# Exponential, row sum and maximum of eight softmaxes moved between two engines, head by head

## The chip, the cores and the metric

The kernel runs on one core of a Trainium2 chip. The metric is the device time of one execution in microseconds (us); the median of three timed runs is 855.88 us (855.29 to 855.99). One further execution was taken with a profile, and all rows below are from it. The engines are named as in the profile: PE is TensorE, DVE is VectorE, ACT is ScalarE, POOL is GpSimd, SP is SyncE. Differences within 0.2% (1.7 us) can't be told from no change.

## The reference, cut to what matters

```python
q_c, k_c, v_c = (x.reshape(B, H, nc, 64, D) for x in (q, k, v))   # B, H, S, D = 8, 8, 576, 64
scores = np.matmul(q_c, k_c.transpose(0, 1, 2, 4, 3)) / np.sqrt(D)
scores = scores - np.max(scores, axis=-1, keepdims=True)
attn = np.exp(scores)
attn = attn / (np.sum(attn, axis=-1, keepdims=True) + 1e-09)
x = np.matmul(attn, v_c)                  # then heads side by side: x is [4608, 512]
h = x @ w_in                              # w_in  [512, 2048]
g = np.maximum(h, 0.0) ** 2
out = g @ w_out                           # w_out [2048, 512]
```

Attention is done within chunks of 64 positions, so each chunk of a head has a softmax of its own over 64 scores. The two weight matrices come as 64-bit floats.

## The kernel before, in words

**Tiling.** Two chunks of all eight heads make a *pair*: 128 rows of `x`. There are 36 pairs, in blocks of 4, 4, 4, 6, 6, 6 and 6. The first eight pairs (class `Pair`; `NN` is 8) are the plain ones; the change touches these alone. The other 28 (class `Quad`) have a softmax of their own code. A value that goes into a large matmul is split in two parts, high and low, and each product takes three matmuls.

**A plain pair.** PE turns q and k (`turn`), and they are copied out of PSUM: q into the block-diagonal tile `qbd`, in two halves of 64 partitions (`keep_q`: by DVE for pairs 0 and 1, by ACT for the others), k into `kt` (`keep_k`, ACT). PE makes the scores in a PSUM bank, 128 rows by 8 heads by 64 (`scores`, tile `sc`). Then `top` (maximum per row and head, tile `nm`), `less` (scores less maximum, tile `ne`), `exps` (one exponential over all 512 columns, in place), `sums` (row sums, tile `nz`), `small` (adds 1e-9), `norm` (reciprocal and product). PE turns the result (`turn_p`), ACT copies it (`keep_p`, tile `tt`), PE multiplies by the values (`values`), ACT writes the high part of `x` and DVE the low part (`place`).

**The lead.** Pairs 0 to 3 are done first. Their `small` is on DVE, and they use banks of their own. Where PE has nothing to do in the lead, `fill` gives it runs of 8 or 16 short matmuls with no use (L393), as the 22 of `heat` at the start do. After pair 3 comes the first large matmul, slice `h0_0` of block 0.

**Block 0.** The first product has 16 slices (`h0_0` to `h0_15`), twelve matmuls each, and the second has 16 of twelve (`o0`), two slices behind (`LAG`). Each slice needs a converted piece of `w_in` or `w_out`: `convert_w` makes the split out of 64-bit words in seven steps, three instructions on ACT (L157, L158, L187) and five on DVE (L163, L169, L175, L182, L197), 32 pieces in all. So in the same stretch ACT and DVE convert weights, square and split `g` (ACT L617, L623, L629; DVE L632), and do the softmax of pairs 4 to 7 (`small` on POOL there).

**What sets the order.** `Plan` holds each step with an engine, a cost, what it reads and writes, and a rank; it plays the plan through with these costs and writes out each engine's instructions in that order. Engines then take their own queue in order and wait on semaphores. A changed cost or step therefore changes the order on every engine up to the end of block 0 and a little beyond.

Of the kernel before, what the change touches and what calls it, by code (L numbers as in the profile page):

```python
# [10 lines left out]
F32 = mybir.dt.float32  # L11
# [3 lines left out]
AF = mybir.ActivationFunctionType  # L15
ALU = mybir.AluOpType
AX = mybir.AxisListType
# [3 lines left out]
def kernel(  # L21
# [20 lines left out]
    nc = tc.nc  # L42
    B, H, S, D = q.shape
    NT, DM = out.shape
    DFF = w_in.shape[1] // 2
    P = 128
    CH = 64
# [4 lines left out]
    QSCALE = 1.0 / math.sqrt(D)  # L52
# [222 lines left out]
    class Quad:  # L275
# [31 lines left out]
        def less(self):  # L307
            self.e = late["pool"].tile([P, HH, 2, CH], F32, name=f"e{self.pair}", tag="e", bufs=1)
            for c in range(2):
                nc.vector.tensor_tensor(  # L310
                    self.e[:, :, c], four[c][:, 0], self.m[:, c].broadcast_to([P, HH, CH]), op=ALU.subtract
                )
# [4 lines left out]
        def sums(self):  # L317
            self.z = att.tile([P, HH, 2, 1], F32, name=f"z{self.pair}", tag="nz", bufs=2)
            nc.vector.tensor_reduce(self.z, self.e, axis=AX.X, op=ALU.add)
            nc.vector.tensor_scalar_add(self.z, self.z, 1e-9)  # L320
            nc.vector.reciprocal(self.z, self.z)
# [73 lines left out]
    class Pair:  # L395
# [36 lines left out]
        def keep_q(self, s):  # L432
            r = halves[s]

            copy = nc.vector.tensor_copy if self.u < 2 else nc.scalar.copy
            copy(qbd[self.u % 2][r, :, s], self.psq[r])

        def keep_k(self):
            self.kt = raw.tile([P, H, CH], F32, name=f"kt{self.u}", tag="qk"[self.u % 2] + "_raw")
# [12 lines left out]

        def top(self):
            self.m = att.tile([P, H, 1], F32, name=f"nm{self.u}", tag="nm", bufs=2)
            nc.vector.tensor_reduce(self.m, self.sc, axis=AX.X, op=ALU.max)

        def less(self):
            self.e = nat.tile([P, H, CH], F32, name=f"ne{self.u}", tag=f"ne{self.u % 2}")
            nc.vector.tensor_tensor(
                self.e, self.sc, self.m.broadcast_to([P, H, CH]), op=ALU.subtract  # L460
            )

        def exps(self):
            nc.scalar.activation(self.e, self.e, AF.Exp, scale=QSCALE)

        def sums(self):
            self.z = att.tile([P, H, 1], F32, name=f"nz{self.u}", tag="nz", bufs=2)
            nc.vector.tensor_reduce(self.z, self.e, axis=AX.X, op=ALU.add)

        def small(self):  # L470
            (nc.vector if self.lead else nc.gpsimd).tensor_scalar_add(self.z, self.z, 1e-9)
# [202 lines left out]
    class Mixed(Step):  # L674
# [30 lines left out]
        def add(self, i, h, side, s):  # L705
            nc.vector.tensor_tensor(self.kept(i)[:, h * HN:(h + 1) * HN], sides[side][:, :HN], snap(s), op=ALU.add)  # L706
# [246 lines left out]
    def program():  # L953
# [4 lines left out]
        add = p.add  # L958
# [41 lines left out]
        def attention(u):  # L1000
            x = prs[u]
            i = u % 2
            if x.lead:
                bq, bk, bs = ("o", 2 * i), ("o", 2 * i + 1), ("h", i)
            else:
                bq, bk, bs = (("at", next(turn_at) % 2) for _ in range(3))
            if 2 <= u < lead:
                bp, bx = bk, bq
            else:
                bp, bx = (("at", next(turn_at) % 2) for _ in range(2))  # L1010
            x.banks = {"q": bq, "k": bk, "sc": bs, "pt": bp, "xt": bx}
            r = ["early"]
            wait = 0.0 if x.lead else SLACK
            add(PE, 4 * 0.11, lambda: x.turn(0), [("q", u), "ident"], [bq], slack=wait)
            for s in range(2):
                e = DVE if u < 2 else ACT
                add(e, ONE, lambda s=s: x.keep_q(s), [bq] + r, [("qbd", i, s)])
            add(PE, 4 * 0.11, lambda: x.turn(1), [("k", u), "ident"], [bk], slack=wait)
            add(ACT, ONE, x.keep_k, [bk] + r, [("raw", "qk"[i])])
            if u in (0, lead - 1):  # L1020
                filler(x, "sc", bs, [bq, bk])
            add(PE, 1.05, x.scores, [("qbd", i, 0), ("qbd", i, 1), ("raw", "qk"[i])] + r, [bs],
                slack=wait)
            add(DVE, TWO, x.top, [bs], [("m", i)])
            add(DVE, TWO, x.less, [bs, ("m", i)] + r, [("e", i)])
            add(ACT, ONE, x.exps, r, [("e", i)])
            add(DVE, TWO, x.sums, [("e", i)] + r, [("z", i)])
            add(DVE if x.lead else POOL, 0.2 if x.lead else 0.41, x.small, [], [("z", i)])
            add(DVE, TWO + 0.2, x.norm, [("z", i)] + r, [("e", i)])
            if u in (0, lead - 1):  # L1030
                filler(x, "pt", bp, [bs])
            add(PE, 4 * 0.11, x.turn_p, [("e", i), "ident"] + r, [bp], slack=wait)
            add(ACT, ONE, x.keep_p, [bp] + r, ["tt"])
            if u in (0, lead - 2, lead - 1):
                filler(x, "xt", bx, [bp])
            add(PE, 1.05, x.values, [("v", slot_of(u)), "tt"] + r, [bx], slack=wait)
            xh, xl = x_names(u, "h"), x_names(u, "l")
            add(ACT, ONE, lambda: x.place(0), [bx], xh)
            add(DVE, TWO, lambda: x.place(1), [bx] + xh, xl)
# [416 lines left out]
```

## Time and profile before

| What | Value |
|---|---|
| median of three runs | 855.88 us |
| the profiled execution | 856.38 us, its span 854.6 us |
| PE busy | 845.0 us (99%) |
| DVE busy | 540.6 us (63%) |
| ACT busy | 367.8 us (43%) |
| POOL busy | 242.5 us (28%) |
| mean granted clock of PE | 0.999 |

The span runs from the first to the last instruction; 1.8 us of the profiled execution lie around it. The profiled execution is 0.5 us above the median. Busy shares are means over the whole span; the plain pairs lie in the first 116 us of it. A matmul's end is modelled in the profile, so PE's share says little by itself.

### The profile page before, as it was taken

The page shows a single profiled execution, that of the slowest core. Times are in us where ns is not written, and L with a number is a line of the kernel's source. Part 1 is how long each engine was busy: PE and PEld are TensorE (multiplying, and loading weights), DVE is VectorE, ACT ScalarE, POOL GpSimd, SP SyncE. Part 2 cuts the span into 40 slices and gives each one's busy share as a digit, 9 for nine tenths or more (in the row PEclk, how much of TensorE's full clock was granted, in tenths as well). Part 3 has the DMA queues.
Part 4 walks back from the last instruction along what each step waited for, and adds up shares of the span by engine and source line. Part 5 has one row for each costly group of instructions (what it writes and reads, how often), then busy time and mean ns, then how long its engine had stood idle before and what let it go on. Part 6 is the DMA issues. An engine that isn't in the chain of part 4 may idle for free.

```text
span 854.6 us, 16517 instructions
## 1 busy us (share of the span) xinstructions
PE 845.0 (99%) x6142; PEld 729.6 (85%) x6142; DVE 540.6 (63%) x962; ACT 367.8 (43%) x669; POOL 242.5 (28%) x432
## 2 busy tenths in 40 slices
PE   9999999999999999999999999999999999999998
PEld 7787878888888888888988988898898888999896
DVE  5999997777775347665586566566656637524233
ACT  4899885444454345232343323243332334222221
POOL 2000006344553122343331434342333222222110
PEclk9999999999999999999999999999999999999999
DMA  7797438666696326966784777674778443745311
GB/s 185 225 267 219 148 87 208 156 157 155 154 302 138 56 56 166 209 154 143 176 185 133 178 181 163 142 180 115 211 152 210 106 96 100 230 111 149 87 49 75
DMA packets 241504, 132.72 MB, mean 155 GB/s; under 512 B 185744, under 2 KB 200336, under 8 KB 241424
## 3 DMA queue, kind: packets, MB, share of 16 engines
q0 software_dynamic: 47360, 80.77, 35.1%
q1 hardware_dynamic: 191808, 50.24, 26.8%
q8 instruction: 49, 0.80, 0.4%
q10 hardware_dynamic: 2256, 0.66, 0.3%
q14 instruction: 31, 0.25, 0.1%
HBM read 103.81 MB, written 24.12 MB: 150 GB/s over the span
## 4 chain that ended last, share of the span: by engine, by line
PE 88%; DVE 10%; issue 1%; POOL 0%; ACT 0%; POOLq 0%; DVEq 0%
PE o L729 31%; PE side L697 28%; PE o L642 12%; PE h L606 11%; PE side L345 2%; PE side L298 2%; DVE wia L175 1%; DVE woa L175 1%; DVE wi L197 1%; DVE wia L182 1%; DVE woa L182 1%; DVE wo L197 1%; DVE wia L163 1%; DVE wia L169 1%; DVE gs L632 1%
## 5 line engine op out<-in xcount | busy, mean ns | idle before, releaser
L697 PE MATMUL side<-xc,ring 128*128 128x384 f32 x1344 | 241.3, 336 | 1.3 <-DVE xc L1240 1.3
L697 PEld LDWEIGHTS side<-xc,ring 128*128 128x128 f32 x1344 | 235.7, 188 | 4.9 <-DVE xc L1240 1.5
L687 POOL DMA_DIRECT2D ring<-combos x224 | 121.8, 544 | 311.1 <-PE side L697 304.0
L706 DVE TENSOR_TENSOR gf<-side,aside 128x384 f32<-128x384 f32 x96 | 53.5, 557 | 170.6 <-PE side L697 166.6
L606 PE MATMUL h<-x,wi 128*128 128x512 f32 x576 | 145.0, 395 | 1.6 <-ACT wi L187 1.0
L729 PE MATMUL o<-wo,gs_f 128*128 128x512 f32 x576 | 142.3, 395 | 0.0
L642 PE MATMUL o<-wo,gs 128*128 128x512 f32 x576 | 141.7, 392 | 0.0
L729 PE MATMUL o<-wo,gs_s 128*128 128x512 f32 x576 | 135.9, 389 | 0.0
L606 PEld LDWEIGHTS h<-x,wi 128*128 128x128 f32 x576 | 106.1, 188 | 26.6 <-DVE wi L197 2.7
L729 PEld LDWEIGHTS o<-wo,gs_s 128*128 128x128 f32 x576 | 108.1, 188 | 22.3
L642 PEld LDWEIGHTS o<-wo,gs 128*128 128x128 f32 x576 | 107.2, 188 | 22.3
L729 PEld LDWEIGHTS o<-wo,gs_f 128*128 128x128 f32 x576 | 106.5, 188 | 21.6
L272 POOL DMA_DIRECT2D v_raw<-in_v_dram x112 | 69.7, 633 | 106.8 <-PE side L345 80.5
L703 ACT COPY aside<-side 128x384 f32<-128x384 f32 x96 | 46.2, 481 | 120.7 <-PE side L697 120.2
L632 DVE TENSOR_TENSOR gs<-g,gs 128x512 fp32r<-128x512 f32 x48 | 32.9, 685 | 44.2 <-ACT gs L629 44.1
L712 DVE SCALAR_TENSOR_TENSOR gf<-gf 128x768 f32<-128x768 f32 x64 | 58.6, 952 | 1.1 <-ACT gf L709 0.9
L719 DVE TENSOR_TENSOR gs_f<-gf,gs_f 128x768 fp32r<-128x768 f32 x32 | 30.0, 937 | 23.7 <-ACT gs_f L715 23.7
L617 ACT ACTIVATE g<-h 128x512 f32<-128x512 f32 x48 | 28.6, 595 | 35.0 <-PE h L606 32.7
L629 ACT CAST gs<-g 128x512 fp32r<-128x512 f32 x48 | 29.7, 620 | 31.7 <-PE o L642 31.3
L709 ACT ACTIVATE gf<-side 128x384 f32<-128x384 f32 x32 | 15.7, 492 | 61.4 <-PE side L697 61.4
L305 DVE TENSOR_REDUCE m<-side 128x4 f32<-128x256 f32 x56 | 21.1, 418 | 30.5 <-ACT aside L357 28.6
L334 ACT COPY p<-et 128x512 f32<-128x512 f32 x28 | 17.4, 622 | 52.2 <-DVE et L328 51.9
(113 smaller groups left out, 846.9 us busy)
## 6 DMA issues: line engine op xcount, KB each, us to landing
ring<-combos POOLq DMA_DIRECT2D x224, 256.0 KB, 3.7
wiraw<-in_moe_w_in_dram SPq DMA_DIRECT2D x16, 512.0 KB, 6.1
woraw<-in_moe_w_out_dram SPq DMA_DIRECT2D x16, 512.0 KB, 5.8
out_dram<-ob SPq DMA_DIRECT2D x30, 256.0 KB, 3.3
q_raw<-in_q_dram SPq DMA_DIRECT2D x224, 32.0 KB, 2.1
k_raw<-in_k_dram SPq DMA_DIRECT2D x224, 32.0 KB, 3.6
v_raw<-in_v_dram POOLq DMA_DIRECT2D x112, 64.0 KB, 2.3
combos<-wi POOLq DMA_DIRECT2D x48, 128.0 KB, 3.1
```

The costliest lines, as they stand in the source:

```text
L272: nc.gpsimd.dma_start(out=t[r, c], in_=s.rearrange("h j d -> j h d"))
L606: nc.tensor.matmul(self.h[:, :self.n], a[:, c], bb[:, c, :self.n], start=c == 0 and i == 0, stop=last,)
L629: nc.scalar.copy(self.gh[:, :self.n], self.g)
L632: nc.vector.tensor_tensor(self.gl[:, :self.n], self.g, self.gh.bitcast(F32)[:, :self.n], op=ALU.subtract)
L642: nc.tensor.matmul(acc[b, j], a[:, j * P:(j + 1) * P], bb, start=f == 0 and i == 0, stop=f == NF - 1 and i == 2,)
L687: nc.gpsimd.dma_start(out=ring(self.m + i).rearrange("p l c n -> p (l c n)"), in_=combos[self.p, i])
L697: nc.tensor.matmul(sides[side][:, :HN], w[:, l, c], part(x, r)[:, c], skip_group_check=True, start=(c, u) == (0, 0) and i in (0, 1, 3), st ...
L703: nc.scalar.copy(snap(i), sides[side][:, :HN])
L706: nc.vector.tensor_tensor(self.kept(i)[:, h * HN:(h + 1) * HN], sides[side][:, :HN], snap(s), op=ALU.add)
L712: nc.vector.scalar_tensor_tensor(self.kept(i), self.kept(i), 0.0, self.kept(i), op0=ALU.max, op1=ALU.mult)
L719: nc.vector.tensor_tensor(l, self.kept(i), h.bitcast(F32), op=ALU.subtract)
L729: nc.tensor.matmul(acc[b, j], a[:, j * P:(j + 1) * P], bb, start=first and u == 0, stop=last and u == 2)
```

## The change: what it does

Of each plain pair, DVE's `less` and `sums` are taken out, two instructions over 128 rows and 512 columns. `exps` becomes eight instructions on ACT, one for each head, 128 rows by 64 columns: each reads the scores from PSUM, adds the head's maximum as a bias per row, takes the exponential, writes `ne`, and writes the row's sum to a column of `nz` (`accum_out`). So that bias and scores have the same scale, q is multiplied by -1/8 as it is copied (`keep_q`: a multiplication on DVE, an activation with a scale on ACT), and `top` takes the minimum of the negated scores. The planner's cost of `exps` goes from 0.61 to 8 times 0.21.

```diff
@@ keep_q
-            copy = nc.vector.tensor_copy if self.u < 2 else nc.scalar.copy
-            copy(qbd[self.u % 2][r, :, s], self.psq[r])
+            to, of = qbd[self.u % 2][r, :, s], self.psq[r]
+            if self.u < 2:
+                nc.vector.tensor_scalar_mul(to, of, -QSCALE)
+            else:
+                nc.scalar.activation(to, of, AF.Copy, scale=-QSCALE)
...
@@ top, less, exps, sums
-            nc.vector.tensor_reduce(self.m, self.sc, axis=AX.X, op=ALU.max)
-
-        def less(self):
+            nc.vector.tensor_reduce(self.m, self.sc, axis=AX.X, op=ALU.min)
+
+        def exps(self):
+
             self.e = nat.tile([P, H, CH], F32, name=f"ne{self.u}", tag=f"ne{self.u % 2}")
-            nc.vector.tensor_tensor(
-                self.e, self.sc, self.m.broadcast_to([P, H, CH]), op=ALU.subtract
-            )
-
-        def exps(self):
-            nc.scalar.activation(self.e, self.e, AF.Exp, scale=QSCALE)
-
-        def sums(self):
             self.z = att.tile([P, H, 1], F32, name=f"nz{self.u}", tag="nz", bufs=2)
-            nc.vector.tensor_reduce(self.z, self.e, axis=AX.X, op=ALU.add)
+            for h in range(H):
+                nc.scalar.activation(
+                    self.e[:, h], self.sc[:, h], AF.Exp, bias=self.m[:, h], scale=-1.0, accum_out=self.z[:, h]
+                )
...
@@ attention
             add(DVE, TWO, x.top, [bs], [("m", i)])
-            add(DVE, TWO, x.less, [bs, ("m", i)] + r, [("e", i)])
-            add(ACT, ONE, x.exps, r, [("e", i)])
-            add(DVE, TWO, x.sums, [("e", i)] + r, [("z", i)])
+            add(ACT, H * 0.21, x.exps, [bs, ("m", i)] + r, [("e", i), ("z", i)])
```

In the rows of order below, the digit in a tile's name is the pair (`kt1` is `kt` of pair 1), `side0`, `side1`, `pt` and `xt` are PSUM banks, and a row with x8 stands for eight equal instructions.

On ACT in the lead, from `keep_k` of pair 0 on, before:

```order
L440 COPY kt0_179<-k0_161 128x512
L440 COPY kt1_220<-k1_204 128x512
L464 ACTIVATE ne0_226<-ne0_226 128x512
L436 COPY qbd0_93<-q2_228 64x8x64 x2
L440 COPY kt2_275<-k2_259 128x512
L436 COPY qbd1_94<-q3_270 64x8x64
L491 COPY tt0_303<-side0_80 128x512
L436 COPY qbd1_94<-q3_270 64x8x64
L464 ACTIVATE ne1_301<-ne1_301 128x512
L440 COPY kt3_324<-k3_306 128x512
L464 ACTIVATE ne2_348<-ne2_348 128x512
```

and now:

```order
L443 COPY kt0_179<-k0_161 128x512
L465 ACTIVATE ne0_220,nz0_221<-sc0_166,nm0_202 128x64 x8
L443 COPY kt1_240<-k1_204 128x512
L439 ACTIVATE qbd0_93<-q2_235 64x8x64 x2
L443 COPY kt2_275<-k2_242 128x512
L490 COPY tt0_288<-side0_80 128x512
L465 ACTIVATE ne1_307,nz1_308<-sc1_251,nm1_281 128x64 x8
L439 ACTIVATE qbd1_94<-q3_283 64x8x64
L465 ACTIVATE ne2_358,nz2_359<-sc2_290,nm2_322 128x64 x8
...
L439 ACTIVATE qbd1_94<-q3_283 64x8x64
L443 COPY kt3_401<-k3_317 128x512
```

The eight instructions of pair 0 stand ahead of `kt1`, which the scores of pair 1 need; those of pairs 1 and 2 stand ahead of `kt3`, which the scores of pair 3 need.

On PE in the lead, from the values of pair 0 on (the rows left out are runs of L393), before:

```order
L500 MATMUL side1_81<-tt0_303,vbd0_95 64x64 x16
...
L448 MATMUL sc3_354<-kt3_324,qbd1_94 64x64 x16
L486 MATMUL side0_80<-ident_88,ne1_301 128x128 x4
...
L500 MATMUL side1_81<-tt1_411,vbd1_96 64x64 x16
L486 MATMUL pt2_444<-ident_88,ne2_348 128x128 x4
```

and now:

```order
L499 MATMUL side1_81<-tt0_288,vbd0_95 64x64 x16
L485 MATMUL side0_80<-ident_88,ne1_307 128x128 x4
...
L485 MATMUL pt2_394<-ident_88,ne2_358 128x128 x4
...
L499 MATMUL side1_81<-tt1_388,vbd1_96 64x64 x16
L451 MATMUL sc3_372<-kt3_401,qbd1_94 64x64 x16
...
L499 MATMUL xt2_403<-tt2_477,vbd2_97 64x64 x16
L485 MATMUL pt3_483<-ident_88,ne3_514 128x128 x4
```

The scores of pair 3 (`sc3`) now stand behind the turned results of pairs 1 and 2 and the values of pair 1, where before they stood ahead of all three. The last row, `pt3`, turns the result of pair 3.

On DVE in block 0, around the softmax of pair 4, before:

```order
L455 TENSOR_REDUCE nm4_763<-side0_80 128x8
L163 TENSOR_SCALAR woa3_753<-woa3_753 128x512
L459 TENSOR_TENSOR ne4_772<-side0_80,nm4_763 128x512
L169 TENSOR_SCALAR woa3_753<-woa3_753 128x512
L163 TENSOR_SCALAR wia5_765<-wia5_765 128x512
L175 SCALAR_TENSOR_TENSOR woa3_753<-woraw3_507,woa3_753 128x512
L169 TENSOR_SCALAR wia5_765<-wia5_765 128x512
L468 TENSOR_REDUCE nz4_791<-ne4_772 128x8
L182 ISA woa3_753<-woraw3_507,woa3_753 128x1024
L474 RECIPROCAL nz4_791<-nz4_791 128x8
```

and now:

```order
L458 TENSOR_REDUCE nm4_789<-side0_80 128x8
L197 TENSOR_TENSOR wi4_783<-wia4_706,wi4_783 128x512
L175 SCALAR_TENSOR_TENSOR woa3_757<-woraw3_525,woa3_757 128x512
L182 ISA woa3_757<-woraw3_525,woa3_757 128x1024
L163 TENSOR_SCALAR wia5_796<-wia5_796 128x512
L169 TENSOR_SCALAR wia5_796<-wia5_796 128x512
L175 SCALAR_TENSOR_TENSOR wia5_796<-wiraw5_528,wia5_796 128x512
L631 TENSOR_TENSOR gs0_3_826<-g0_3_780,gs0_3_826 128x512
L473 RECIPROCAL nz4_807<-nz4_807 128x8
L474 TENSOR_TENSOR ne4_806<-ne4_806,nz4_807 128x512
L197 TENSOR_TENSOR wo3_833<-woa3_757,wo3_833 128x512
```

Between the maximum and the reciprocal of pair 4, DVE now has seven instructions of weights and of `g`, and neither L459 nor L468; the reciprocal waits for POOL's addition, and this for the last of ACT's eight heads. Behind it stands the last step of `wo3`.

## Rows read from the trace of the kernel before

**Rows 1.** Busy us of each engine in three stretches of the first 116 us.

```profile
core 0: us, PE busy (x) PEld busy (x) DVE busy (x) ACT busy (x) POOL busy (x), PEclk, DMA share, GB/s
5.00:31.35 26.35, 25.20 (x382) 21.48 (x380) 21.68 (x43) 15.80 (x29) 1.65 (x2) 1.00 0.83 226
31.35:41.36 10.01, 8.86 (x37) 6.71 (x37) 9.94 (x20) 9.20 (x17) 0.00 (x0) 1.00 0.64 163
41.36:116.00 74.64, 74.22 (x559) 59.44 (x557) 73.44 (x142) 66.50 (x121) 2.43 (x4) 1.00 0.67 207
```

**Rows 2.** Chain that ended last, in order: start us, us, what.

```profile
22.39 0.60 DVE ne L459
...
115.53 0.61 DVE wi L197
116.19 2.56 PE h L606 x10
...
136.19 2.72 PE o L642 x12
```

**Rows 3.** Groups by line and form on DVE, to 125 us: busy us, mean ns.

```profile
L468 DVE TENSOR_REDUCE nz<-ne 128x8 f32<-128x512 f32 x8 | 5.4, 680 | 0.3 <-ACT ne L464 0.2
L436 DVE COPY qbd<-q 64x512 f32<-64x512 f32 x4 | 2.8, 688 | 7.2 <-PE q L425 7.2
L459 DVE TENSOR_TENSOR ne<-sc,nm 128x512 f32<-128x512 f32 x4 | 2.7, 683 | 0.0
```

**Rows 4.** Groups by line and form on ACT, to 125 us.

```profile
L617 ACT ACTIVATE g<-h 128x512 f32<-128x512 f32 x14 | 8.4, 598 | 2.4 <-DVE gs L632 1.5 <-PE h L606 0.9
...
L464 ACT ACTIVATE ne<-ne 128x512 f32<-128x512 f32 x8 | 5.0, 630 | 1.1 <-DVE ne L459 1.1
...
L963 ACT ACTIVATE warm<-ident 128x1 f32<-128x1 f32 x1 | 0.2, 203 | 0.0
```

**Rows 5.** ACT in order of time: start us, us.

```profile
14.35 0.59 ACT L440 COPY kt<-k 128x512 f32<-128x512 f32 x1 [0.88 <-PE k L425]
14.84 0.58 ACT L436 COPY qbd<-q 64x512 f32<-64x512 f32 x1
...
50.34 0.63 ACT L464 ACTIVATE ne<-ne 128x512 f32<-128x512 f32 x1
50.88 0.62 ACT L623 ACTIVATE g<-g 128x512 f32<-128x512 f32 x1
```

**Rows 6.** DVE in order of time.

```profile
9.81 0.69 DVE L455 TENSOR_REDUCE nm<-sc 128x8 f32<-128x512 f32 x1 [1.24 <-PE sc L448]
...
13.23 0.17 DVE L471 TENSOR_SCALAR nz<-nz 128x8 f32<-128x8 f32 x1
...
13.67 0.69 DVE L475 TENSOR_TENSOR ne<-ne,nz 128x512 f32<-128x512 f32 x1
...
38.23 0.69 DVE L197 TENSOR_TENSOR wi<-wia,wi 128x512 fp32r<-128x512 f32 x1
```

**Rows 7.** PE in order of time.

```profile
1.35 4.87 PE L968 MATMUL side<-ident 128*128 128x256 bf16 x22 [1.35 <-POOL ident masks.py:199]
...
23.78 1.91 PE L393 MATMUL xt<-ident 128*128 128x256 bf16 x16
25.62 1.15 PE L500 MATMUL xt<-tt,vbd 128*64 128x64 f32 x32
27.75 0.66 PE L486 MATMUL pt<-ident,ne 128*128 128x128 f32 x4 [0.97 <-DVE ne L475]
...
30.29 1.05 PE L393 MATMUL h<-ident 128*128 128x256 bf16 x8
31.35 5.74 PE L606 MATMUL h<-x,wi 128*128 128x512 f32 x24
38.06 0.73 PE L606 MATMUL h<-x,wi 128*128 128x512 f32 x2 [0.97 <-ACT wi L187]
...
41.36 0.85 PE L642 MATMUL o<-wo,gs 128*128 128x512 f32 x3
```

## The prediction

> **What bounds the kernel now.** I read the chain that ended last first. In its pieces up to 116 us DVE stands nearly everywhere (softmax, weight conversion); the piece at 115.53 us is its last, and from 116.19 us PE follows at 2.72 us for twelve large matmuls [rows 2]. So the plain pairs lie in the only part of the run whose chain is not PE's. A chain names the engine that came last, however, not how far the next one was behind. For that I read the busy times by stretch [rows 1]. In the lead (5.00 to 31.35 us) no engine is full: DVE 21.68 and ACT 15.80 of 26.35 us; the four pairs wait on one another there. In block 0, from 41.36 to 116 us, PE is busy 74.22, DVE 73.44 and ACT 66.50 of 74.64 us. PE is thus full there too, DVE just keeps pace, and ACT has 8.1 us left. Between the two, PE makes three slices of twelve from 31.35 to 41.36 us, 10.0 us where 3 x 2.72 = 8.2 would do, waiting 0.97 us of it visibly for a weight [rows 7], and DVE is at 9.94 of 10.01 us. What DVE gives back can be won in two places: in the start of the first large matmul (31.35 us), and in those 1.85 us. After 41 us there is under a microsecond of PE's idle time to win.
>
> **What goes from DVE.** L459 and L468, 0.68 us each [rows 3], eight of each: 10.9 us of DVE's work. In the lead, DVE's part between maximum and normalization falls out of the path of each pair, but with it the place where the maximum was applied is now ACT's.
>
> **What comes to ACT: the price of one head.** The exponential of 512 columns out of SBUF takes 0.63 us, and the next instruction starts 0.54 us later [rows 4, 5]. Nothing in the trace has 64 columns, a bias per row, or a row sum. From one column to 512 an exponential goes from 203 to 630 ns [rows 4], so a column costs 0.84 ns, 64 cost 54, and an instruction of 64 columns would take 0.256 us. Lower bound: a copy of 512 columns out of PSUM starts 0.49 us before the next [rows 5], of which 0.43 are columns; that leaves 0.06, and 0.06 + 0.05 = 0.11 us a head, if bias and sum are free. Upper bound: 0.256 us without overlap and one more one-column instruction for the sum, 0.203 us: 0.46 us. I take the nearest row, the one-column exponential, for the sum too, each with the overlap of 0.09 us (0.63 less 0.54) that ACT shows: 0.256 + 0.203 - 0.18 = 0.28 us a head, 2.24 us for eight, 2.34 to the end of the last.
>
> The Trainium skill (ScalarE: Activation LUTs, What ACT_TABLE_LOAD costs) gives an activation with a bias per row as about 280 ns + 0.833 ns a column, and an overlap of 93 ns back to back. The overlap agrees with the 0.09 us of [rows 5]; for the bias no run here shows it. By it a head would be an estimated 0.24 us without its sum, and the total below would come out 1.3 us lower. The skill also holds (Perfetto Trace Analysis, Optimizing Scalar/DVE Operations) that an engine near saturation gains by grouping work in larger instructions, which speaks against this change, ACT having 8.1 of 74.64 us to spare.
>
> **Multiplication as q is copied.** On ACT an activation out of PSUM takes 0.598 us against 0.58 to 0.59 for a copy [rows 4, 5]: 12 x 0.02 us, spread over the pairs. On DVE the trace has no multiplication out of PSUM; between that copy's 0.69 us [rows 3] and a third less, it lies at the start, where DVE waits for PE. Both at nothing.
>
> **The lead, step by step.** The maximum of pair 0 ends at 9.81 + 0.69 = 10.50 us [rows 6], as before. Now ACT makes eight heads, 10.55 to 12.90. `kt1` stands behind them (to 13.40), where it used to be first; so the scores of pair 1 end at 14.6 and their minimum at 15.3. ACT then does `tt0`, and pair 1's heads run from 15.70 to 18.05, one copy of q to 18.45, and pair 2's heads to 20.80. Addition, reciprocal and product on DVE take 1.13 us (13.23 to 14.36, [rows 6]) and a hop: 22.0. PE turns pair 2 (some 0.5 us), runs the 16 fillers queued there (1.84, from 23.78 to 25.62, [rows 7]), makes the values of pair 1 (1.15 less an overlap of ends, 1.1) and only then, in as much time, the scores of pair 3, which end at 26.7. The minimum of pair 3 stands on DVE behind the low part of `x` of pair 1 and ends at 27.5; its heads end at 29.90, its product at 31.1. From the turning of pair 3 (27.75) to the first large matmul (31.35) it is 3.60 us before [rows 7], and the same steps follow now: 31.15 + 3.60 = 34.75 us. That is **3.4 us later**, with four blocks of eight heads in the path, so that each 0.01 us a head moves it by 0.32 us.
>
> **What is given back at once.** The three first slices need the weight `wi2`, whose low part started at 38.23 us before [rows 6] and held PE. Now DVE, freed of L459 and L468 and past the softmax at 31.1 us, has 18 instructions up to and with that low part (seven of 0.34 and eleven of 0.60 us from start to start, 9.0 us, and a wait of 0.2 for ACT's last copy into `x`) and ends it at some 40.3 us; the third slice starts at 34.75 + 2 x 2.72 = 40.2 us and needs the low part in its third matmul. So the slices take 8.2 us instead of 10.0: 1.85 us less, and the second product starts at 42.9 instead of 41.36 us: **1.55 us later**.
>
> **Block 0.** Each of pairs 4 to 7 adds 2.24 - 0.54 = 1.7 us to ACT: 6.8 of the 8.1 us it had. DVE has 4 x 2 x 0.60 = 4.8 us less to do. ACT then stands where DVE stood, at 98%, with the relu, the square and the high part of `g` and the high parts of weights queued behind each block of eight. DVE gets a new wait as well: its reciprocal waits for POOL and this for the eighth head, and the low part of the next weight stands behind it; its 4.8 us cover 1.2 us a pair. PE would wait now and then, as it did for DVE. Bounds: nothing, if the order hides it all, and 2 us, if ACT, starting late by the same 1.5 us, fills its queue. I take 0.9 us. From 116 us on PE sets the pace, and a delay stays as it is.
>
> **Sum.** 3.4 - 1.85 + 0.9 = +2.45 us on the profiled execution's 856.38 us (span 854.6 and 1.8 around it): 858.8. That run lies 0.5 us above the median of 855.88, so the forecast for the median is 858.3 us, 0.3% slower.
>
> **Rivals.**
>
> *Faster: a head for 0.17 us.* If bias and sum cost nothing and only the overlap counts, a head takes 0.256 - 0.09 = 0.17 us, 1.33 for eight. The path in the lead shrinks by 4 x 0.9 = 3.5 us: the first large matmul starts at 31.2, the 1.85 us come back in full, and ACT has room (4 x 0.8 = 3.2 of 8.1 us), so that block 0 costs nothing. -0.1 - 1.85 = -2.0 us: 853.9. It decides at some 0.18 us a head. For it speaks that reading PSUM is cheaper on ACT than reading SBUF (0.49 against 0.54 us from start to start, [rows 5]); against it, that it needs two free extras. With the lower bound of 0.11 it would be another 1 to 2 us.
>
> *No difference: a head for 0.21 us*, the planner's own number. The lead ends 4 x 8 x 0.07 = 2.2 us earlier than in my sum, at 32.5 us; with 1.85 back and 0.3 for block 0 it is about -0.4 us: 855.5. For it speaks that the planner's other costs lie near the rows (0.61 for rows of 0.58 to 0.63).
>
> *Much slower: ACT runs out.* At 0.35 us a head the lead starts 5.6 us late; pairs 4 to 7 want 4 x 2.26 = 9.0 us where 8.1 are, and the excess goes to PE on top of the 0.9: 5.6 - 1.85 + 1.8 = +5.6, 861.4 us. At the upper bound of 0.46 it is some +12 us. Here belongs PE's clock. The 22 short matmuls at the start take 4.87 us, 0.22 each, and eight such later 1.05 us, 0.12 each [rows 7]: PE starts at the lower of its two levels, 1.2 GHz, though the granted clock reads 1.00. In the order now, PE has nothing between the values of pair 2 (end 28.9) and the turning of pair 3 (31.15), 2.3 us against 0.97 before. If the clock fell there, the 3.6 us that follow could last up to twice as long.
>
> The Trainium skill (TensorE: Matmul & The Clock Gate, What's actually happening) has PE return to 1.2 GHz after it was idle; whether this wait suffices no row shows.
>
> **How the numbers follow.** The forecast (0.255 to 0.33 us a head, +1.7 to +4.7 us) gets 0.38, no difference 0.31, faster 0.17, much slower 0.14. Slower by over 0.2% (what a measurement can tell) is then the forecast and the last rival, 0.52; within it 0.31; faster 0.17. The range leaves about one in ten on each side: down to 853.2, into the faster rival, and up to 862.3, past 0.35 us a head. The likeliest case alone spans 857.6 to 860.6.
>
> **What would show it.** Groups by line: the time from the first to the eighth head divided by seven is the price; 0.28 is mine, and a second row per head would be the sum's own instruction. PE in order of time: first large matmul at 34.7 us, second product at 42.9, no wait for `wi2`, a wait of over 2 us before pair 3 is turned. ACT's busy time in block 0 near 98%, DVE's at 92 to 95%. It is wrong if the heads cost under 0.2 us, if some other order of arrival takes the heads out of the path of the lead, or if block 0 starts late and catches up, for which PE would have to have idle time there that its modelled ends hide.

## The result, and the profile after

The changed kernel takes 860.19 us (median of four runs, 859.94 to 860.66); the kernel before, run beside it, 855.93 us (855.29 to 856.70). The ratio is 1.0052, with a 95% interval of 1.0037 to 1.0067: 0.5% slower. The profiled execution took 860.28 us, its span 858.3 us, 3.7 us longer than that of before.

What a head costs stands in the groups by line and form of ACT in the first 125 us (line, engine, operation, tiles, shapes, count, busy us and mean ns, then the idle time before them). They answer to [rows 4]:

```profile
L465 ACT ACTIVATE ne<-sc,nm 128x64 f32<-128x64 f32 x32 | 9.5, 330 | 2.8 <-DVE nm L458 2.8
L465 ACT ACTIVATE ne<-side,nm 128x64 f32<-128x64 f32 x32 | 9.5, 328 | 0.6 <-DVE nm L458 0.6
...
L465 ACT ACTIVATION_READ_ACCUMULATOR ne<-sc,nm 128x1 f32 x32 | 7.2, 224 | 0.0
L465 ACT ACTIVATION_READ_ACCUMULATOR ne<-side,nm 128x1 f32 x32 | 7.1, 221 | 0.0
```

Each head has two rows: the activation, and a second instruction that reads the row sum out of the accumulator. What both take from start to start shows in ACT in order of time (start, duration, then the group; in brackets the wait before it), where [rows 5] had one exponential for all heads:

```profile
9.85 0.31 ACT L465 ACTIVATE ne<-sc,nm 128x64 f32<-128x64 f32 x1 [2.43 <-DVE nm L458]
10.06 0.19 ACT L465 ACTIVATION_READ_ACCUMULATOR ne<-sc,nm 128x1 f32 x1
10.15 0.30 ACT L465 ACTIVATE ne<-sc,nm 128x64 f32<-128x64 f32 x1
...
12.17 0.62 ACT L443 COPY kt<-k 128x512 f32<-128x512 f32 x1
```

Eight heads hold ACT from 9.85 to 12.17: 2.32 us, 0.29 a head (some 0.20 for the activation, 0.09 for the read-out).

PE in order of time, which answers to [rows 7]:

```profile
12.85 1.15 PE L451 MATMUL sc<-kt,qbd 128*64 128x64 f32 x32 [0.99 <-ACT kt L443]
...
21.68 0.63 PE L485 MATMUL pt<-ident,ne 128*128 128x128 f32 x4 [1.28 <-DVE ne L474]
...
30.94 0.63 PE L485 MATMUL pt<-ident,ne 128*128 128x128 f32 x4 [2.81 <-DVE ne L474]
...
34.41 8.46 PE L605 MATMUL h<-x,wi 128*128 128x512 f32 x36
42.70 0.85 PE L641 MATMUL o<-wo,gs 128*128 128x512 f32 x3
...
325.35 0.87 PE L696 MATMUL side<-xc,ring 128*128 128x384 f32 x4
```

The scores of pair 1 now wait for `kt1`, which stands behind the eight heads of pair 0; the turning of pair 3 waits 2.81 us. The 36 matmuls of the first three slices, on the other hand, run through without a wait for `wi2`. The last row is the first of L696, with which a part of the program begins that the change leaves alone.

The windows of lead, slices and block 0 (length, then busy us and count of PE, PE's weight loads, DVE, ACT and POOL, the granted clock, the DMA share, GB/s), as in [rows 1]:

```profile
5.00:34.41 29.41, 24.07 (x383) 20.61 (x381) 18.61 (x38) 23.77 (x90) 1.65 (x2) 1.00 0.88 244
34.41:42.70 8.29, 8.29 (x37) 6.86 (x37) 8.26 (x18) 7.53 (x14) 0.00 (x0) 1.00 0.75 229
42.70:116.00 73.30, 70.33 (x541) 56.04 (x540) 69.11 (x130) 71.05 (x178) 1.15 (x4) 1.00 0.64 192
```

In block 0 ACT has gone to 97% (71.05 of 73.30 us), DVE to 94%, and PE, which had 0.42 us idle there, has 2.97. What it waited for up to 135 us (total, times, longest):

```profile
PE pt L485 <- DVE ne L474: 4.1, 2, 2.8
PE side L485 <- DVE ne L474: 2.1, 2, 1.8
...
PE sc L451 <- ACT kt L443: 1.0, 1, 1.0
PE side L499 <- ACT tt L490: 0.7, 1, 0.7
PE h L605 <- DVE wi L197: 0.4, 1, 0.4
```

The 1.8 us are pair 6: its minimum ends at 86.40 us on DVE, but its heads start at 87.65, behind two word pieces and a relu on ACT, the last read-out ends at 90.1, POOL adds 1e-9 at 90.17, DVE's product starts at 90.68, and PE turns it at 91.52.

**Five marks.** The start of pair 0's maximum on DVE moves from one profiled execution to the next with the length of the 22 short matmuls at the start (3.97 to 4.88 us), and everything behind it moves along. So I measure from that start: to the first large matmul (lead), from there to the second product (slices), from there to the first row of L696 (block 0 and what follows it), and from there to the end. Us, one profiled execution each; the last columns are the difference of the first three to before, and the timed ratio to before.

| kernel | lead | slices | block 0 on | to the end | sum of three against before | ratio |
|---|---|---|---|---|---|---|
| before | 21.54 | 10.01 | 280.39 | 532.85 | | |
| the change | 25.29 | 8.29 | 282.65 | 532.95 | +4.29 | 1.0052 |
| lead_only | 25.29 | 8.29 | 281.56 | 531.94 | +3.20 | 1.0031 |
| late_only | 21.54 | 10.04 | 279.81 | 532.00 | -0.55 | 0.9990 |
| late_start | 24.66 | 9.70 | 280.33 | 532.58 | +2.75 | 1.0031 |
| removal_only | 19.65 | 9.48 | 279.23 | 531.99 | -3.58 | 0.9955 |
| sums_dve | 21.42 | 10.27 | 281.46 | 532.56 | +1.21 | 1.0007 |
| no_bias | 22.35 | 8.33 | 281.18 | 534.22 | -0.08 | 1.0013 |
| row_max | 19.98 | 10.01 | 280.13 | 532.56 | -1.82 | 0.9971 |
| true_cost | 25.64 | 9.21 | 281.63 | 532.64 | +4.54 | 1.0057 |
| k_first | 22.36 | 10.49 | 283.44 | 532.56 | +4.35 | 1.0045 |
| turn_later | 25.28 | 8.30 | 286.20 | 532.59 | +7.84 | 1.0097 |
| row_lead | 19.96 | 10.02 | 284.82 | 532.04 | +2.86 | 1.0030 |
| pay_aside | 23.92 | 9.81 | 287.26 | 536.42 | +9.05 | 1.0154 |

The change, then, costs 3.75 us in the lead, gets 1.72 back in the slices, and loses 2.26 behind them. The column to the end scatters by 2.3 us (531.94 to 534.22, pay_aside apart) in code that is the same in all. What makes that stays open, so a difference of the sums under 1 us says little.

### The profile page after: what moved, and what is told of

Its sections match the earlier page's. It is cut to its first block, busy times and chain, and to the rows that moved or that the text cites. A ratio compares the mean times of both kernels' runs of the same rounds, so it can differ in the third digit from the quotient of the medians.

```text
span 858.3 us, 16630 instructions
## 1 busy us (share of the span) xinstructions
PE 842.3 (98%) x6142; PEld 728.9 (85%) x6142; DVE 533.6 (62%) x946; ACT 381.5 (44%) x789; POOL 240.7 (28%) x432
## 4 chain that ended last, share of the span: by engine, by line
PE 88%; SPq 3%; DVE 3%; ACT 3%; DMA 2%; issue 1%; POOL 0%; POOLq 0%; ACTq 0%
PE o L728 31%; PE side L696 27%; PE o L641 13%; PE h L605 13%; PE side L345 2%; PE side L298 2%; DMA wiraw<-in_moe_w_in_dram 1%; SPq L230 1%; SPq L260 1%; ACT ne L465 1%; SPq L144 0%; DMA qk_raw<-in_q_dram 0%; DMA vbd<-in_v_dram 0%; DVE gs L631 0%; SPq L142 0%
## 5 line engine op out<-in xcount | busy, mean ns | idle before, releaser
L696 PE MATMUL side<-xc,ring 128*128 128x384 f32 x1344 | 240.6, 336 | 1.3 <-DVE xc L1237 1.3
L696 PEld LDWEIGHTS side<-xc,ring 128*128 128x128 f32 x1344 | 235.7, 188 | 4.2 <-DVE xc L1237 1.5
```

The source lines that it names most:

```text
L696: nc.tensor.matmul(sides[side][:, :HN], w[:, l, c], part(x, r)[:, c], skip_group_check=True, start=(c, u) == (0, 0) and i in (0, 1, 3), st ...
```

## The experiments

My theory: ACT's eight heads are the price, paid at once in the lead, where each block of eight lies in the path from pair to pair, and in block 0 in ACT's scarce room. The rival: the price as such would be hidden, and what costs is the order, which the planner makes with a head at 0.21 us. A second question came up with the first runs: whether block 0 loses by its late start or by its own late pairs.

### Where the loss is made: lead, late pairs, a late start

`lead_only` does the change on pairs 0 to 3 alone, `late_only` on pairs 4 to 7 alone:

```diff
+    def heads(u):
+        return u < blocks[0]            # late_only: u >= blocks[0]
...
+            if heads(u):
                 add(ACT, H * 0.21, x.exps, [bs, ("m", i)] + r, [("e", i), ("z", i)])
+            else:
+                add(DVE, TWO, x.less, [bs, ("m", i)] + r, [("e", i)])
+                add(ACT, ONE, x.exps_all, r, [("e", i)])
+                add(DVE, TWO, x.sums, [("e", i)] + r, [("z", i)])
```

> Pairs 0 to 3 as in the change, pairs 4 to 7 as before. Theory A (the price of a head, 0.29 us, is paid in the path of the lead, and again on ACT in block 0): the first large matmul some 3.4 us later than before, 1.85 us of it given back by the three first slices, nothing lost in block 0: 1.2 to 2.2 us slower than before. Theory B (not the price, but the order that the planner makes with a cost that is too low, is what costs): most of the loss sits where PE was found waiting in block 0, so this run is within 0.8 us of before.

> Pairs 0 to 3 as before, pairs 4 to 7 as in the change. Theory A: ACT at 97% in block 0 with queues behind each block of eight heads: 1.0 to 2.5 us slower than before, with a wait of PE of over 1 us for the softmax of one pair. Theory B: the same, 2 to 4 us. If the freed time of DVE were worth more than the price on ACT there, it would be faster than before by up to 1 us.

Measured: lead_only 858.23 against 855.22 us, 1.0031 [1.0020, 1.0043], more than the 1.2 to 2.2 us of theory A; late_only 854.75, 0.9990 [0.9981, 0.9998]. Lead and slices of lead_only are to the hundredth those of the change. Of the 1.72 us that the slices give back, 1.17 are lost again further on, though the pairs there are those of before; PE's waits between 40 and 135 us are for converted weights:

```profile
PE h L623 <- DVE wi L197: 1.0, 2, 0.5
PE h L623 <- ACT wi L187: 0.3, 1, 0.3
```

The engine that is full there is DVE, with the subtraction and the sums of pairs 4 to 7 back on it: 73.94 us busy of the 75.00 behind the second product.

```profile
42.30:117.30 75.00, 74.20 (x559) 59.66 (x558) 73.94 (x142) 67.55 (x122) 2.49 (x4) 1.00 0.67 201
```

late_only was to cost something by my account of block 0, and did not. The window of 75 us from its second product on:

```profile
40.09:115.09 75.00, 74.67 (x561) 60.12 (x560) 71.89 (x138) 74.42 (x184) 0.93 (x4) 1.00 0.68 207
```

ACT is busy 74.42 of 75.00 us, and PE loses 0.33 in all. So a full ACT alone isn't what costs time in block 0.

`late_start` is the kernel before, with 31 more short matmuls ahead of the first large one, so that block 0 begins late and nothing else changes:

```diff
-                    warm_up(self.h, WARM_P)
+                    warm_up(self.h, WARM_P + 31)
```

> The kernel before with 31 more short matmuls of no use ahead of the first large one (3.75 us at 0.121 each, as much as the lead lost with the change), and nothing else. It tells what a late start alone is worth while ACT and DVE go on with weights. Theory A as first told (the start is late, 1.7 us are given back at once): 1.5 to 2.2 us slower than before, and the rest of block 0 as before. Theory D (the 1.7 us are only lent: PE then meets the weights' pace later in block 0): 2.5 to 3.5 us slower, as with the change in the lead alone.

Measured: 858.37 against 855.77 us, 1.0031 [1.0019, 1.0043]. The 2.6 us lie in the range of theory D, but not by its mechanism: the first large matmul came 3.12 us later, 0.31 came back in the slices, and block 0 ran as before (280.33 against 280.39), so nothing was lent.

The run doesn't tell what a late start is worth to engines that go on with the weights, because they didn't go on. The planner does not count the 31 matmuls, so the order on ACT is that of before, with the relu of the first slice (L617) ahead of the next word pieces. ACT stands idle for that relu, DVE waits 1.98 us for ACT, and the low part of `wi2` comes late as well (ACT, then DVE):

```profile
37.53 0.60 ACT L617 ACTIVATE g<-h 128x512 f32<-128x512 f32 x1 [3.02 <-PE h L606]
...
41.05 0.68 DVE L197 TENSOR_TENSOR wi<-wia,wi 128x512 fp32r<-128x512 f32 x1
```

and the same row in the change:

```profile
39.47 0.69 DVE L197 TENSOR_TENSOR wi<-wia,wi 128x512 fp32r<-128x512 f32 x1
```

Counted from the first maximum, this row starts at 28.42 us before, at 31.22 in late_start (2.80 later) and at 30.35 in the change (1.93 later). The slices give back by how much more PE's start moved than this row: 3.12 - 2.80 = 0.32 us here (0.31 measured), 3.75 - 1.93 = 1.82 in the change (1.72). In the change four instructions on words of weights stand on ACT from 35.76 us until the first relu at 38.03. How much of the 1.72 us is due to that order, and how much to DVE being freed of L459 and L468, these runs don't separate. Of block 0's 2.26 us, 1.17 come already from the changed lead with the old late pairs; the late pairs add the rest there, and alone they cost nothing.

### What the removal is worth without its price

`removal_only` keeps the maximum but does not subtract it, takes one exponential of 512 columns out of PSUM, and leaves the row sums out (the maximum stands in for them):

```diff
-            for h in range(H):
-                nc.scalar.activation(
-                    self.e[:, h], self.sc[:, h], AF.Exp, bias=self.m[:, h], scale=-1.0, accum_out=self.z[:, h]
-                )
+            nc.scalar.activation(self.e, self.sc, AF.Exp, scale=-1.0)
...
```

> The two DVE instructions are gone and nothing comes to ACT: one exponential of 512 columns out of PSUM; the maximum is made but not subtracted, and the row sum is left out (the maximum stands in its place in the normalization). Theory A: what DVE gives back is worth something by itself, in the lead (0.6 us or more a pair in its path) and in the 1.85 us before the second product: 1.5 to 4 us faster than before. Theory C (PE is full from 31 us on and the lead has other limits, so the removal is worth nothing, and the whole price shows): within 0.8 us of before.

Measured: 851.62 against 855.22 us, 0.9955 [0.9942, 0.9967]. Taking DVE's two instructions out is worth 3.6 us, as long as ACT's part stays one instruction. That one holds ACT for 0.49 us here:

```profile
10.58 0.60 ACT L464 ACTIVATE ne<-sc 128x512 f32<-128x512 f32 x1 [2.42 <-DVE nm L458]
11.07 0.58 ACT L443 COPY kt<-k 128x512 f32<-128x512 f32 x1
```

So ACT's eight heads cost 3.58 + 4.29 = 7.9 us, for 8 x (2.32 - 0.49) = 14.6 us more work on ACT. More than half of what is put on ACT reaches the end.

`pay_aside` was to price that work off the path: removal_only, and beside it the eight heads into a tile that nothing reads:

```diff
...
+            add(ACT, H * 0.21, x.aside, [bs, ("m", i)] + r, ["da"])
```

> The two DVE instructions gone and one exponential of 512 columns out of PSUM, as in the run of the removal alone, and beside it, on ACT, the change's eight heads with bias and row sum, written where nobody reads (in bfloat16), so that ACT pays the price but no softmax waits for it; maximum not subtracted, row sum left out of the result. If ACT's time is what costs (its queue, and the weights behind it): 2 to 5 us slower than before. If the path of each softmax through the heads is what costs: within 1 us of before, or faster.

Measured: 868.91 against 855.77 us, 1.0154 [1.0137, 1.0171], far above what either theory gave, and not for a reason that either had. PE in order of time, long after the plain pairs, in pay_aside:

```profile
151.49 2.96 PE L646 MATMUL o<-wo,gs 128*128 128x512 f32 x12
154.30 2.96 PE L610 MATMUL h<-x,wi 128*128 128x512 f32 x12
157.09 2.96 PE L646 MATMUL o<-wo,gs 128*128 128x512 f32 x12
```

and in removal_only:

```profile
158.29 2.88 PE L602 MATMUL h<-x,wi 128*128 128x512 f32 x12
161.01 2.88 PE L638 MATMUL o<-wo,gs 128*128 128x512 f32 x12
163.73 2.88 PE L602 MATMUL h<-x,wi 128*128 128x512 f32 x12
```

Twelve large matmuls start 2.80 us apart, where they start 2.72 us apart in every other kernel here, at a granted clock of 1.00 in both and with no wait shown. The new tile may move others in SBUF; whether that is the cause was not tried. The run says nothing on the price of the heads.

### What a head's price is made of

`sums_dve` leaves the row sums to DVE, as before, and keeps eight activations with a bias; `no_bias` keeps the sums on ACT and leaves the bias out (the maximum is then found and not used):

```diff
 sums_dve
-                    self.e[:, h], self.sc[:, h], AF.Exp, bias=self.m[:, h], scale=-1.0, accum_out=self.z[:, h]
+                    self.e[:, h], self.sc[:, h], AF.Exp, bias=self.m[:, h], scale=-1.0
...
+            nc.vector.tensor_reduce(self.z, self.e, axis=AX.X, op=ALU.add)
 no_bias
-                    self.e[:, h], self.sc[:, h], AF.Exp, bias=self.m[:, h], scale=-1.0, accum_out=self.z[:, h]
+                    self.e[:, h], self.sc[:, h], AF.Exp, scale=-1.0, accum_out=self.z[:, h]
```

> Eight heads on ACT with the maximum as bias, but without the row sum; the sum is one instruction on DVE as before. A head then costs 0.20 us instead of 0.29 (the row of the sum's read-out falls away), 0.74 us less for eight, and DVE's sum of 0.7 us comes back into the path of each pair. Theory A: the lead as long as with the change, within 0.6 us; 3 to 5 us slower than before. If the sum on ACT were what costs, it would be under 2 us slower.

> Eight heads on ACT with the row sum, but without the bias: the maximum is made and not subtracted (the same softmax, since the normalization divides it out). Theory A, with a bias per row costing some 0.09 us: a head costs 0.20 us, the lead is 4 x 0.74 = 3.0 us shorter than with the change, and the run is within 1.5 us of before. If the bias is free, a head stays at 0.29 us and the run at 3.5 to 5 us slower.

Measured: sums_dve 856.54 against 855.87 us, 1.0007 [0.9997, 1.0016]; no_bias 857.17, 1.0013 [1.0004, 1.0023]. For sums_dve I had expected 3 to 5 us more, with a lead as long as the change's; 0.7 came, and the lead is 3.87 us shorter. Not all of that is the price of the sum, because the plan differs too: PE makes the scores of pair 3 (19.74 us) ahead of the turning of pair 2 (21.76), where the change has them behind it (24.97 and 21.68). ACT in order of time has eight heads from 9.61 to 11.20, 0.20 us a head and no second row.

```profile
9.61 1.75 ACT L464 ACTIVATE ne<-sc,nm 128x64 f32<-128x64 f32 x8 [2.43 <-DVE nm L458]
11.20 0.63 ACT L443 COPY kt<-k 128x512 f32<-128x512 f32 x1
```

In no_bias the groups of ACT in the first 125 us have the shorter activation:

```profile
L465 ACT ACTIVATE ne<-sc 128x64 f32<-128x64 f32 x32 | 6.6, 243 | 2.8 <-DVE nm L458 2.8
...
L465 ACT ACTIVATION_READ_ACCUMULATOR ne<-sc 128x1 f32 x32 | 6.5, 229 | 0.0
```

Its eight heads run from 9.94 to 11.53, 0.198 us each. This run keeps the change's plan and alters nothing but the price; its lead is 2.94 us shorter than the change's, about four times the 0.73 us that eight heads got cheaper. So of the 0.29 us of a head the read-out of the sum is 0.09, the bias per row 0.09, and the activation itself 0.10. Either of the first two out, and the change is within 0.2% of before. The Trainium skill (ScalarE: Activation LUTs, What ACT_TABLE_LOAD costs) gives an activation with a bias per row as about 280 ns + 0.833 ns a column, by which 64 columns take an estimated 333 ns, and each such operand as about 93 ns; the rows agree (328 to 330 ns, and 0.29 - 0.198 = 0.09 us).

`row_max` pays the bias once a pair: one maximum per row over all eight heads, one activation of 512 columns with it as bias, sums on DVE. (A softmax doesn't change by what is subtracted from a row, as long as no head's scores lie so far below the common maximum that their exponentials vanish.)

```diff
+                self.m[:, 0], self.sc.rearrange("p h j -> p (h j)"), axis=AX.X, op=ALU.min
...
+            nc.scalar.activation(self.e, self.sc, AF.Exp, bias=self.m[:, 0], scale=-1.0)
...
+            nc.vector.tensor_reduce(self.z, self.e, axis=AX.X, op=ALU.add)
```

> One maximum per row over all eight heads in place of one per head (the softmax is the same, the normalization divides it out): one activation of 512 columns out of PSUM with that bias; row sums on DVE as before. Only DVE's subtraction goes, at a price of some 0.1 us on ACT. Theory A (the price per instruction, eight times, is what made the change slow): faster than before by 1 to 3 us. Theory C (removal is worth nothing): within 0.8 us of before.

Measured: 853.49 against 855.87 us, 0.9971 [0.9958, 0.9983], faster than both kernels. ACT in order of time:

```profile
9.45 0.69 ACT L465 ACTIVATE ne<-sc,nm 128x512 f32<-128x512 f32 x1 [2.39 <-DVE nm L458]
10.04 0.58 ACT L443 COPY kt<-k 128x512 f32<-128x512 f32 x1
```

The one activation holds ACT for 0.59 us, where the exponential out of SBUF without a bias held it for 0.54 [rows 5] and eight heads 2.32, and `less` is gone from DVE; the lead ends 1.56 us earlier.

### Is it the order, or the planner's number?

The planner counts a head as 0.21 us, and the chip takes 0.29. `true_cost` gives it 0.29; `k_first` moves the copies of k ahead of the heads in the lead, so that the scores of pair 1 don't wait; `turn_later` puts the turning of pairs 4 to 7 2.5 us later in PE's queue.

```diff
 true_cost
-            add(ACT, H * 0.21, x.exps, [bs, ("m", i)] + r, [("e", i), ("z", i)])
+            add(ACT, H * 0.29, x.exps, [bs, ("m", i)] + r, [("e", i), ("z", i)])
 k_first
+            rank, p.rank = p.rank, -16 if x.lead else p.rank
             add(ACT, ONE, x.keep_k, [bk] + r, [("raw", "qk"[i])])
+            p.rank = rank
 turn_later
+            late = 0.0 if x.lead else SLACK + 2.5
-            add(PE, 4 * 0.11, x.turn_p, [("e", i), "ident"] + r, [bp], slack=wait)
+            add(PE, 4 * 0.11, x.turn_p, [("e", i), "ident"] + r, [bp], slack=late)
```

> The change with the planner's cost of a head raised from 0.21 to the measured 0.29 us; the instructions are the same, their order is not. Theory A: the lead pays as much (first large matmul at 34 to 35 us), the waits of PE in block 0 shrink by 1 to 2 us: 2 to 3.5 us slower than before. Theory B: with the right cost the loss goes: within 0.8 us of before.

> The change with the copies of k of pairs 0 to 3 ranked ahead of everything else on ACT: the copy of pair 1 stands ahead of pair 0's eight heads, and the scores of pair 3 ahead of the turned results of pair 2. Theory A (ACT's time for the heads is the price, wherever it stands): the lead gets shorter, but the weights then wait behind the heads, and the three first slices take over 10 us: 1.5 to 3.5 us slower than before. Theory B (it is the place in the queue, heads ahead of the copies of k, that costs): the loss goes, within 0.8 us of before.

> The change, with one number in the planner altered: the turning of the exponentials of pairs 4 to 7 (turn_p outside the lead) is placed in PE's queue 2.5 us later than now, so that PE has large matmuls to do until the softmax is ready. Lead and the first three slices should stay as in the change. Theory A (ACT has too little room in block 0; a wait at one place is only its form): PE's wait of 1.82 us for pair 6 goes, but waits for converted weights of about the same sum (1 to 2 us) come in its place, as they did with the planner's cost at 0.29; block 0 stays 1.6 to 2.8 us later than before, and the time is 0.3% to 0.6% above before (858.5 to 861). Theory B (the turn stands too early in PE's queue, and that is what block 0 loses): the wait goes and nothing takes its place; block 0 loses under 0.8 us, and the time falls to 857.5 to 858.3, 0.2% to 0.28% above before.

Measured: true_cost 860.16 against 855.22 us, 1.0057 [1.0043, 1.0071]; k_first 860.12 against 855.87, 1.0045 [1.0030, 1.0060]; turn_later 863.49 against 855.80, 1.0097 [1.0081, 1.0114]. None of the three recovers anything, and true_cost and k_first, 4.9 and 4.3 us slower, lie above the 3.5 us of theory A as well. In true_cost the wait for pair 6's softmax is all but gone and waits for weights stand in its place (PE's waits from 40 to 135 us):

```profile
PE h L605 <- ACT wi L187: 1.3, 1, 1.3
PE h L605 <- DVE wi L197: 0.9, 2, 0.8
PE side L485 <- DVE ne L474: 0.2, 1, 0.2
```

In k_first the lead is only 0.82 us longer than before, but the slices take 10.49 us and block 0 loses 3.05. Most of PE's waits there, from 40 to 135 us, are for the softmax of two late pairs:

```profile
PE side L485 <- DVE ne L474: 2.2, 2, 1.7
```

In turn_later the wait of 1.8 us goes, and PE waits instead for weights up to 140 us:

```profile
PE h L605 <- DVE wi L197: 2.0, 4, 1.4
...
PE h L605 <- ACT wi L187: 1.3, 2, 1.0
```

So theory B falls: the wait goes, and others come. But the time lies 2.5 us above the upper end of theory A. PE in order of time, and the windows there, show the rest:

```profile
107.19 0.50 PE L605 MATMUL h<-x,wi 128*128 128x512 f32 x1 [1.40 <-DVE wi L197]
107.62 1.95 PE L451 MATMUL side<-kt,qbd 128*64 128x64 f32 x32
```

```profile
106.00:108.00 2.00, 0.81 (x9) 0.57 (x11) 2.00 (x4) 1.03 (x2) 0.00 (x0) 0.92 0.68 217
108.00:110.00 2.00, 2.00 (x31) 1.88 (x28) 0.73 (x2) 0.00 (x0) 0.00 (x0) 0.50 1.06 381
110.00:112.00 2.00, 2.00 (x8) 1.53 (x7) 0.30 (x1) 1.67 (x12) 0.00 (x0) 0.72 1.02 368
```

Behind the wait of 1.40 us the granted clock falls to 0.50, the lower level of 1.2 GHz, and the 32 score matmuls take 1.95 us instead of 1.15. These scores are the next pair's, so its minimum and its heads come later too: ACT stands idle for 3.30 us before they start at 110.33.

`row_lead` has row_max in the lead and the change's heads, at 0.29 in the plan, in pairs 4 to 7:

```diff
+            if x.lead:
+                add(ACT, ONE + 0.08, x.exps, [bs, ("m", i)] + r, [("e", i)])
+                add(DVE, TWO, x.sums, [("e", i)] + r, [("z", i)])
+            else:
+                add(ACT, H * 0.29, x.exps, [bs, ("m", i)] + r, [("e", i), ("z", i)])
```

> Pairs 0 to 3 with one maximum per row over all heads and one activation of 512 columns with that bias (row sums on DVE), pairs 4 to 7 with the change's eight heads (planned at 0.29 us each). If late heads cost only where block 0 starts late: as fast as with the row's maximum everywhere or up to 0.8 us faster, 2 to 3.5 us faster than before. If they cost by themselves: 0 to 1.5 us faster than before.

Measured: 858.19 against 855.77 us, 1.0030 [1.0020, 1.0040]. Both theories had it faster than before, by 0 to 3.5 us; it is 2.4 us slower, although the lead ends 1.58 us earlier. Block 0 loses 4.43 us, most of it at one place. PE in order of time there, and the windows around it:

```profile
74.85 1.09 PE L497 MATMUL side<-ident,ne 128*128 128x128 f32 x4 [3.51 <-DVE ne L486]
75.59 3.44 PE L617 MATMUL h<-x,wi 128*128 128x512 f32 x9
```

```profile
74.00:76.00 2.00, 1.15 (x5) 1.18 (x6) 1.99 (x4) 1.36 (x4) 0.00 (x0) 0.65 0.00 0
76.00:78.00 2.00, 2.00 (x6) 1.52 (x6) 1.93 (x4) 2.00 (x5) 0.00 (x0) 0.50 0.00 0
```

PE waits 3.51 us for the softmax of a late pair (its heads stand behind a relu, a square and word pieces on ACT), then runs at 0.50 of the clock, and nine large matmuls take 3.44 us. Late heads are thus harmless or dear by where the plan happens to put the turn: free in late_only, over 4 us here. What tells the cases apart is how many large matmuls PE has, in order of time, between the scores of a late pair and its turning. At this place there are 12. There are 18 at pair 6 of the change, at the same pair of no_bias and at both waits of k_first (1.82, 1.48, 1.69 and 0.56 us waited), and 21 or more, without a wait for the softmax, at all four late pairs of late_only.

## Why the prediction was right, point by point

**The price of a head: right in its sum, by luck in its parts.** 0.28 us was forecast, from a one-column exponential for the sum and nothing for the bias beyond the instruction itself; 0.29 was measured. The sum's second row is there, at 0.09 us from start to start instead of 0.11 (0.203 - 0.09). But the parts were not mine: reading 64 columns out of PSUM costs 0.10, not 0.17 us, and the bias another 0.09. Two errors cancelled; the size of the sum held.

**The lead: right.** 3.4 us were forecast, 3.75 measured from the same mark. Its form is the forecast's: the scores of pair 1 start behind `kt1` behind eight heads, and the turning of pair 3 comes 21.82 us after the first maximum started, where my sum had 31.15 - 9.81 = 21.34. The wait before it, 2.3 us in my sum, is 2.81; the clock did not fall in it (the four matmuls behind it take 0.63 us, and the granted clock is 1.00).

**What is given back in the slices: right.** 1.85 us forecast, 1.72 measured, and no wait for `wi2`, whose low part was forecast to end at some 40.3 us and ended at 40.16. The reason given, that DVE is freed, is not shown by itself: the low part of `wi2` comes 1.93 us later than before, counted from the first maximum, and the slices gain because PE starts later still.

**Block 0: the step that was off.** I took +0.9 us between bounds of 0 and 2, and it was +2.26. Of the 1.9 us between the forecast of 858.3 and the 860.19 measured this term is 1.4; lead and slices add 0.35 and 0.13. The row at fault is the 8.1 us of room that I gave ACT in block 0, and the clause that DVE's gain covers 1.2 us a pair: a sum of busy times doesn't say when a pair's softmax is ready. late_only shows the room to be enough, with ACT at 99%, and row_lead loses 4.43 us with the same late heads and an earlier start. In the change, pair 6 has 18 large matmuls between its scores and its turning, and PE waits 1.82 us. The other part stands in lead_only: with the late pairs of before, 1.17 of the 1.72 us of the slices are gone again once PE needs the next weights, with DVE full. I had added the terms as if each stage's gain were kept. Which ACT instruction is the first to be late in the change was followed for pair 6 alone, and whether the two parts simply add up was not tried. true_cost, k_first and turn_later don't undo the loss; their waits only change their place.

**The rivals.** *Faster* fell with the price: 0.17 us a head was not to be had with a bias and a sum. *No difference at 0.21 us a head* is what no_bias shows at 0.198: lead +0.81 where that rival had 1.15, slices -1.68 for -1.85, block 0 +0.79 for 0.3, in all -0.1 us by the marks and +0.13% in the timed runs. The point from which the price decides was placed about rightly. *Much slower* did not come for the change, but the fall of PE's clock that it names did, in block 0 of turn_later and row_lead: a wait and then PE at 1.2 GHz.

Eight biased heads without sums take 8 x 0.20 = 1.6 us, one biased activation of the same 512 columns 0.59 (9.45 to 10.04 in row_max); with the sums on DVE in both, the kernels take 856.54 and 853.49 us. The Trainium skill (Perfetto Trace Analysis, Optimizing Scalar/DVE Operations), cited against the change, says that grouping work in larger operations can raise the throughput of a saturated engine; these runs agree with it.

## What to carry to other kernels

Count a fused operand as an instruction until a row shows otherwise: here a row sum was a second row of 0.09 us, and a bias per row another 0.09, for each of 64 pieces, and these fixed parts, not the columns, decided between a gain of 0.3% (one biased activation a pair) and a loss of 0.5% (eight). Work that leaves one engine for another should be priced on the one it goes to, in the stretch where that engine is fullest, and then by when its result is due there: the same late heads made PE wait not at all in late_only, with 21 or more large matmuls between a pair's scores and its turning, 1.8 us with 18 in the change and 3.5 with 12 in row_lead. And time given back early is booked only up to the next wait: in lead_only 1.17 of 1.72 us were gone by then, in waits for weights from the very engine that had been freed in the lead.

## What was not expected of the hardware

- An activation with a row sum leaves two rows on ACT, and the read-out, one column wide, takes 0.19 to 0.25 us in its row but 0.09 from start to start.
- Waits of 1.82 and 2.81 us in the change left the granted clock of PE at 1.00. One of 1.40 us in turn_later was followed by 0.50, and so was one of 3.51 us in row_lead. The length of the one wait doesn't tell which it will be.
- The same large matmuls, twelve at a time, took 2.80 us from start to start in pay_aside and 2.72 in the other kernels, at a granted clock of 1.00. The cause stays open.
